# Spreading the weight conversion over the attention pairs of a fused attention, mixer and FFT kernel: fewer steps in pairs 6 to 10, more in the last pair and in the two iterations without scores

## The chip, the cores and the metric

The kernel runs on one core of a Trainium2 chip. The metric is the device time of one execution in microseconds, as the median of several runs. The engines of the core are named as the profile names them: PE is TensorE (matmul, and PEld its weight loads), DVE is VectorE, ACT is ScalarE, POOL is GpSimd, and SP is SyncE, which issues the DMAs.

## The reference

```python
x = attention(q, k, v)      # batch 2, 12 heads, 448 positions, head dim 64, causal, exact softmax
x = moe(x)                  # token mixing 448->256->448 (w_tok1, w_tok2), channel MLP 768->1536->768
x = moe2(x)                 # x + Re(FFT2(x)), layer norm, channel MLP 768->3072->768

def _attn_ref(q, k, v):
    scores = scale * np.matmul(q, k.transpose(0, 1, 3, 2))
    scores = np.where(mask, -1e9, scores)
    attn = softmax(scores)
    return np.matmul(attn, v)

def _moe_ref(x, w_tok1, w_tok2, w_ch1, w_ch2):
    xt = x.transpose(0, 2, 1)
    h = np.maximum(xt @ w_tok1, 0.0) @ w_tok2
    u = x + h.transpose(0, 2, 1)
    h2 = np.maximum(u @ w_ch1, 0.0) @ w_ch2
    return u + h2
```

(Shortened here; the mean and the variance of the layer norm and the two FFTs lie behind the part that the change touches.) The weights reach the kernel as 64-bit floats, and are turned into pairs of 32-bit values (a high part and the rest), with which each product is made in three passes.

## The kernel before

**Attention.** The 12 heads of each of the two batches are taken two at a time: 12 pairs. One loop over n = 0 to 13 is a pipeline of three stages: iteration n makes the scores of pair n (`scores`, PE L261, mask L274, the row maxima on DVE L278, the exps on ACT L287), the transposes of the probabilities of pair n-1 (`transposes`, PE L300, copied out by ACT L305 and DVE L307), and the product with v of pair n-2 (`pv`, PE L315, ACT L320) with its scaling (`finish`, DVE L332, L333, PE L336, DVE L338, L344, POOL L345). `prep` loads and splits q and k of the next pair (ACT L229, L231, POOL L230, DVE L235). In iterations 12 and 13 there are no scores left ("iterations without scores").

**Token mixing inside the same loop.** After every third finished pair, five pieces of token mixing are put on a list, and `next_mix`, called twice an iteration, does the next one: `mix_in` (PE L361, then ACT L367 and DVE L368) with `channels_first` (PE L373, ACT L376), and `mix_out` (PE L395, DVE L397), after which `split` (ACT L401, POOL L402) makes the halves for the channel MLP. The mix_in pieces fall in iterations 5, 8 and 11, and after the loop.

**The channel MLP's beginning.** `early_up(0)` to `early_up(3)` in iterations 12 and 13 are the first four chunks of the MLP's first product (PE L162 to L164, then ACT L165 makes gh, DVE L166 gl), and `early_down(0)` and `early_down(1)` behind the loop the first of its second product (PE L179 to L181 over the four gh and gl, DVE L185). They need weights that have been converted: wa0 to wa3 for early_up, wb0 and wb3 for early_down.

**The conversion.** `convert_steps` turns one tensor of 64-bit words into wh and wl: ACT L83 (m from the words), DVE L85 and L86, DVE L90, DVE L94, ACT L100 (wh), POOL L101 (wl). The generator `converting` does that for eight sources in turn (w1, w2, wa0 to wa3, wb0, wb3), each in three steps, 24 in all: a first with L85 and L86, a second with L90 and with the L83 of the following source, and a third with L94, L100 and L101, after which the source after next is fetched (SP L74) into the buffer of 64-bit words that L94 has just read for the last time. There are two such buffers. wa tensors are 128 x 768, wb tensors 128 x 512.

**What sets the order.** Inside the loop PE runs in the order of the code. The other engines' instructions are put in order by the framework at build time, and each engine then runs its own queue in that order. `weights(after)` does one step of the conversion, to be issued after the instructions given to it. The table `parts` (L461) says how many steps iteration n does; in the pairs' iterations one stands after the first scores, and one more, if there are two, after the third transposes:

```python
parts = [0, 0, 1, 1] + 7 * [2] + [2, 3, 3]
...
if live and parts[n] > 1:
    weights(mark[2:4])
if not live:
    for _ in range(parts[n]):
        weights(mark[:2])
```

Once the loop is over, the rest of the MLP's weights come by the same `convert_steps`, two sources at a time, in the order in which the products need them: wb[0,1] and wb[0,4] are the first two of these.

Of the kernel before, what the change touches and what calls it, by code (L numbers as in the profile page):

```python
# [43 lines left out]
def fused_kernel(ctx: ExitStack, tc: tile.TileContext, qk, v, w1, w2, wa, wb, wc, wd, fa, fa0, fb, out):  # L44
# [27 lines left out]
    def fetch(src):  # L72
        w = stage_pool[0].tile(list(src.shape), I64, tag="w", name="w", bufs=2)
        nc.sync.dma_start(out=w, in_=src)  # L74
        return w
# [111 lines left out]
    with ExitStack() as actx:  # L187
# [24 lines left out]
        mark = [None] * 4  # L212
# [8 lines left out]
        def prep(n):  # L221
            c = Pair()
            pairs[n] = c
            b, hp = n // 6, n % 6
            c.kh, c.kl, c.qh, c.ql = [kq.tile([128, S], F32R, tag=t, name=t) for t in ("kh", "kl", "qh", "ql")]
            k32, q32 = stage(n), stage(n)
            nc.sync.dma_start(out=k32, in_=qk[b, hp, :, 1])
            nc.sync.dma_start(out=q32, in_=qk[b, hp, :, 0])
            act.copy(c.kh, k32)  # L229
            (pool if n else vec).tensor_tensor(out=c.kl, in0=k32, in1=f(c.kh), op=ALU.subtract)  # L230
            act.activation(out=c.qh, in_=q32, func=AF.Copy, scale=0.125)  # L231
            with ExitStack() as order:
                if n == 1:
                    order.enter_context(tc.issue_after(mark[2]))
                vec.scalar_tensor_tensor(  # L235
                    out=c.ql, in0=q32, scalar=0.125, in1=f(c.qh), op0=ALU.mult, op1=ALU.subtract
                )

        def load_v(n):
            pairs[n].v = ap.tile([TS, NI, 2 * D], F32, tag="v", name="v")  # L240
            nc.sync.dma_start(out=pairs[n].v, in_=v[n // 6, n % 6])
# [50 lines left out]
        def transposes(n, u):  # L292
            c = pairs[n]
            if u == 0:
                c.pt = ap.tile([TS, 5, S], F32, tag="pt", name="pt", bufs=1)
            tv = ybank()
            col = 0
            for e, j in (((0, 0),), ((1, 0),), ((0, 1), (0, 3)), ((1, 1), (1, 3)), ((0, 2), (1, 2)))[u]:
                for i in range(j, NI):
                    nc.tensor.transpose(  # L300
                        tv[:TS, col : col + TS], c.p[:, e, OFF[i] + j * TS : OFF[i] + (j + 1) * TS], ident[:TS, :TS]
                    )
                    col += TS
            if u in (1, 3):
                mark[1] = act.copy(c.pt[:, u], tv[:TS, :S]).ins  # L305
            else:
                mark[0] = vec.tensor_copy(c.pt[:, u], tv[:TS, :S]).ins  # L307

        def pv(n):
            c = pairs[n]  # L310
            c.ot = ybank()
            for j in range(NI):
                for e in range(2):
                    u, col = ((e, 0), (2 + e, 0), (4, 224 * e), (2 + e, 336))[j]
                    mm(  # L315
                        c.ot[D * e : D * e + D, j * TS : S], lhsT=c.v[:, j, D * e : D * e + D],
                        rhs=c.pt[:, u, col : col + TS * (NI - j)], start=j == 0, stop=j == NI - 1,
                    )
            c.ots = ap.tile([128, S], F32, tag="ots", name="ots")
            return act.copy(c.ots, c.ot[:, :S]).ins  # L320
# [86 lines left out]
        def next_mix():  # L407
            if mix:
                fn, n, k = mix.pop(0)
                fn(n, k)  # L410
                if fn is mix_out and k == 2:
                    for x in late:
                        split(*x)
                    late.clear()
# [34 lines left out]
        def early_up(fm):  # L449
            up_chunk(None, fm, ahead[fm], (0,), g0, sbank)  # L450

        def early_down(x):
            down_tile([ahead[4 + x]], g0, 0, add_resid, EARLY_DOWN[x], sbank)

        def weights(after):
            with ExitStack() as order:
                for ins in after:
                    order.enter_context(tc.issue_after(ins))
                next(work, None)

        parts = [0, 0, 1, 1] + 7 * [2] + [2, 3, 3]  # L461

        prep(0)
        with tc.manual_schedule(engines={mybir.EngineType.PE}):
            for n in range(np_ + 2):
                live, old = n < np_, 1 <= n <= np_
                if live:
                    scores(n, 0)
                if n + 1 < np_:
                    prep(n + 1)  # L470
                if n in (1, 2):
                    raw.append(fetch(sources[n - 1][0]))
                after = mark[2:4]
                if n >= 2:
                    after.append(pv(n - 2))
                if live and parts[n]:
                    weights(after)
                if live:
                    load_v(n)
                    scores(n, 1)  # L480
                if old:
                    transposes(n - 1, 0)
                    transposes(n - 1, 1)
                next_mix()
                if n == np_:
                    early_up(0)
                if old:
                    transposes(n - 1, 2)
                if live and parts[n] > 1:
                    weights(mark[2:4])  # L490
                if not live:
                    for _ in range(parts[n]):
                        weights(mark[:2])
                if live:
                    scores(n, 2)
                if old:
                    transposes(n - 1, 3)
                    transposes(n - 1, 4)
                if n == np_:
                    early_up(1)  # L500
                next_mix()
                if n == np_ + 1:
                    early_up(2)
                if n >= 2:
                    finish(n - 2)
                if n == np_ + 1:
                    early_up(3)
                if n >= 2 and (n - 2) % 3 == 2:
                    hn = (n - 2) // 3
                    mix += [(mix_first, hn, 0), (mix_second, hn, 1)] + [(mix_out, hn, pr) for pr in range(3)]  # L510
            early_down(0)
            while mix:
                next_mix()
            early_down(1)
# [352 lines left out]
```

## Time and profile before

| | before |
|---|---|
| median of 3 runs | 718.05 us (717.93 to 719.1) |
| the profiled execution's own time | 717.51 us |
| its span | 715.70 us |
| PE busy | 695.1 us (97% of the span) |
| DVE busy | 526.6 us (74%) |
| ACT busy | 282.8 us (40%) |
| POOL busy | 276.7 us (39%) |
| chain that ended last | PE 81%, DVE 10%, ACT 5% |
| fetches of the 64-bit wa and wb tensors, median to landing | 4.3 us and 3.3 us |

The span is what the profiler recorded between the first and the last instruction, and the execution's own time is 1.81 us longer. PE is busy nearly all the time, so the chain of work that ended last runs mostly over PE; a change on another engine counts where PE waits for it. The attention takes about the first 150 us.

### The profile page before, as it was taken

What the parts mean: (1) busy time and instruction counts of PE and PEld (TensorE: products, weight loads), DVE (VectorE), ACT (ScalarE), POOL (GpSimd) and SP (SyncE); (2) the same over time, 40 slices, a digit from 0 to 9 for tenths busy, and PEclk for the clock granted to TensorE, in tenths of its full rate; (3) what the DMA queues carried; (4) which work ended last, traced back from release to release, by engine and by line L of the source; (5) the groups of instructions that cost most, each with busy time, mean ns of one, the idle gap of its engine ahead of it and who ended that gap; (6) DMA issues with size and microseconds to landing.
All of it is one profiled execution on the core that took longest, in us unless ns stands there. A gap on an engine that the chain in (4) does not pass through costs nothing.

```text
span 715.7 us, 10290 instructions
## 1 busy us (share of the span) xinstructions
PE 695.1 (97%) x3940; PEld 629.0 (88%) x3940; DVE 526.6 (74%) x808; ACT 282.8 (40%) x600; POOL 276.7 (39%) x197
## 2 busy tenths in 40 slices
PE   6989899999999999999799999999999999999997
PEld 5677787899999999998699999999999999999996
DVE  6899898554898884779879896767855676944722
ACT  7867777323324333133444452233432323432200
POOL 3235553345332422332195335465313556311210
PEclk9999999999999999999999999999999999999999
DMA  8232412128434342200022442433412343322311
GB/s 265 69 116 96 147 35 82 59 69 224 170 119 147 118 146 90 89 1 0 1 89 88 125 140 90 138 127 118 144 62 81 126 140 126 118 88 95 105 51 52
DMA packets 20608, 74.15 MB, mean 104 GB/s; under 512 B 2364, under 2 KB 6974, under 8 KB 20192
## 3 DMA queue, kind: packets, MB, share of 16 engines
q1 hardware_dynamic: 19952, 69.48, 29.5%
q0 software_dynamic: 608, 4.03, 2.1%
q8 instruction: 31, 0.51, 0.3%
q14 instruction: 17, 0.14, 0.1%
HBM read 70.75 MB, written 2.75 MB: 103 GB/s over the span
## 4 chain that ended last, share of the span: by engine, by line
PE 81%; DVE 10%; ACT 5%; issue 2%; POOL 1%; DMA 0%; ACTq 0%; POOLq 0%; DVEq 0%
PE psum L164 12%; PE psum L163 12%; PE psum L162 12%; PE psum L181 11%; PE psum L180 11%; PE psum L179 11%; PE psum L261 3%; ACT p L287 2%; PE psum L315 2%; PE psum L300 2%; PE psum L395 2%; PE psum L361 1%; DVE nmx L278 1%; DVE resid L655 1%; POOL wl L101 1%
## 5 line engine op out<-in xcount | busy, mean ns | idle before, releaser
L101 POOL TENSOR_TENSOR wl<-m,wh 128x512 fp32r<-128x512 f32 (+1 forms) x90 | 150.1, 1668 | 257.2 <-ACT wh L100 240.6
L180 PE MATMUL psum<-gh,wl 128*128 128x448 f32 x432 | 156.6, 363 | 0.0
L163 PE MATMUL psum<-acth,wl 128*128 128x448 f32 x432 | 156.6, 363 | 0.0
L164 PE MATMUL psum<-actl,wh 128*128 128x448 f32 x432 | 156.4, 362 | 0.0
L181 PE MATMUL psum<-gl,wh 128*128 128x448 f32 x432 | 156.4, 362 | 0.0
L162 PE MATMUL psum<-acth,wh 128*128 128x448 f32 x432 | 156.2, 361 | 0.0
L179 PE MATMUL psum<-gh,wh 128*128 128x448 f32 x432 | 156.2, 361 | 0.0
L83 ACT ACTIVATE m<-w 128x512 f32<-128x512 f32 (+2 forms) x92 | 71.3, 775 | 164.5 <-POOL wl L101 123.1
L85 DVE TENSOR_SCALAR m<-m 128x512 f32<-128x512 f32 (+2 forms) x92 | 48.8, 532 | 77.7 <-ACT m L83 77.6
L90 DVE SCALAR_TENSOR_TENSOR m<-w,m 128x512 uint32<-128x512 uint32 (+2 forms) x92 | 101.6, 1105 | 2.4
L94 DVE SCALAR_TENSOR_TENSOR m<-w,m 128x512 uint32<-128x512 uint32 (+2 forms) x92 | 98.8, 1075 | 1.6
L100 ACT CAST wh<-m 128x512 fp32r<-128x512 f32 (+1 forms) x90 | 63.4, 704 | 90.5 <-DVE m L94 50.2
L162 PEld LDWEIGHTS psum<-acth,wh 128*128 128x128 f32 x432 | 80.9, 187 | 5.8
L163 PEld LDWEIGHTS psum<-acth,wl 128*128 128x128 f32 x432 | 81.1, 188 | 5.6
L180 PEld LDWEIGHTS psum<-gh,wl 128*128 128x128 f32 x432 | 81.1, 188 | 5.6
L179 PEld LDWEIGHTS psum<-gh,wh 128*128 128x128 f32 x432 | 80.9, 187 | 5.8
L164 PEld LDWEIGHTS psum<-actl,wh 128*128 128x128 f32 x432 | 81.0, 188 | 4.8
L181 PEld LDWEIGHTS psum<-gl,wh 128*128 128x128 f32 x432 | 81.0, 187 | 4.8
L166 DVE SCALAR_TENSOR_TENSOR gl<-psum,gh 128x448 fp32r<-128x448 f32 x72 | 43.9, 616 | 25.1 <-ACT gh L165 25.1
L165 ACT ACTIVATE gh<-psum 128x448 fp32r<-128x448 f32 x72 | 37.6, 539 | 61.7 <-PE psum L164 61.7
L86 DVE TENSOR_SCALAR m<-m 128x512 uint32<-128x512 uint32 (+2 forms) x92 | 54.7, 596 | 2.3
L287 ACT ACTIVATE p<-psum,nmx 112x112 f32<-112x112 f32 (+3 forms) x96 | 46.9, 508 | 24.0 <-DVE nmx L278 23.1
(151 smaller groups left out, 855.2 us busy)
## 6 DMA issues: line engine op xcount, KB each, us to landing
w<-in_wc SPq DMA_DIRECT2D x24, 768.0 KB, 4.3
w<-in_wd SPq DMA_DIRECT2D x36, 512.0 KB, 3.4
w<-in_wa SPq DMA_DIRECT2D x12, 768.0 KB, 4.3
w<-in_wb SPq DMA_DIRECT2D x18, 512.0 KB, 3.3
resid<-in_qk SPq DMA_DIRECT2D x24, 224.0 KB, 2.7
v<-in_v SPq DMA_DIRECT2D x12, 224.0 KB, 3.1
out<-t SPq DMA_DIRECT2D x12, 224.0 KB, 1.9
w<-in_w SPq DMA_DIRECT2D x2, 896.0 KB, 9.8
```

The lines of the kernel that those rows point to most:

```text
L83: act.activation(out=m, in_=hi.bitcast(F32), func=AF.Abs)
L90: vec.scalar_tensor_tensor(out=mu, in0=lo, scalar=29, in1=mu, op0=ALU.logical_shift_right, op1=ALU.bitwise_or)
L94: vec.scalar_tensor_tensor(out=mu, in0=hi, scalar=0xC0000000, in1=mu, op0=ALU.bitwise_and, op1=ALU.bitwise_or)
L100: act.copy(wh, m)
L101: pool.tensor_tensor(out=wl, in0=m, in1=f(wh), op=ALU.subtract)
L162: mm(pb[:, :S], lhsT=lh, rhs=act_h[ct][b], start=ct == 0, stop=False)
L163: mm(pb[:, :S], lhsT=ll, rhs=act_h[ct][b], start=False, stop=False)
L164: tail[0] = mm(pb[:, :S], lhsT=lh, rhs=act_l[ct][b], start=False, stop=ct == NCT - 1).ins
L179: mm(pb[:, :S], lhsT=lh, rhs=gh, start=j + k == 0, stop=False)
L180: mm(pb[:, :S], lhsT=ll, rhs=gh, start=False, stop=False)
L181: tail[0] = mm(pb[:, :S], lhsT=lh, rhs=gl, start=False, stop=j == last and k == nk - 1).ins
L287: mark[3] = act.activation(out=c.p[:, e, OFF[i] : OFF[i] + w], in_=se[e][:, c0 : c0 + w], func=AF.Exp, bias=c.nmx[:, i, e], scale=1.0, acc ...
```

## The change

Only the table of the steps and the loop that reads it are changed. The sum stays 24.

| iteration n | 2 | 3 | 4 | 5 | 6 | 7 | 8 | 9 | 10 | 11 | 12 | 13 |
|---|---|---|---|---|---|---|---|---|---|---|---|---|
| steps before | 1 | 1 | 2 | 2 | 2 | 2 | 2 | 2 | 2 | 2 | 3 | 3 |
| steps after | 1 | 1 | 2 | 2 | 1 | 1 | 1 | 1 | 1 | 4 | 6 | 3 |
| done by then, before | 1 | 2 | 4 | 6 | 8 | 10 | 12 | 14 | 16 | 18 | 21 | 24 |
| done by then, after | 1 | 2 | 4 | 6 | 7 | 8 | 9 | 10 | 11 | 15 | 21 | 24 |

```diff
-        parts = [0, 0, 1, 1] + 7 * [2] + [2, 3, 3]
+        parts = [0, 0, 1, 1, 2, 2] + 5 * [1] + [4, 6, 3]
...
-                if live and parts[n] > 1:
-                    weights(mark[2:4])
+                if live:
+                    for _ in range(parts[n] - 1):
+                        weights(mark[2:4])
```

PE's order stays as it was; those of ACT, DVE, POOL and SP change. Three places are shown, with the tiles' numbers.

ACT in iteration 8, up to the L367 of the first half's mix_in there, before; the m and wh tiles are those of the conversion:

```order
L287 ACTIVATE p_1097,ssum_1095<-psum_124,nmx_1096 112x224 x2
L320 COPY ots_1138<-psum_124 128x448
L83 ACTIVATE m_1141<-w_1012 128x768
L305 COPY pt_1158<-psum_124 112x448
L287 ACTIVATE p_1097,ssum_1095<-psum_124,nmx_1096 112x336 x2
L100 CAST wh_1194<-m_921 128x768
L367 ACTIVATE acth4_1_99<-psum_124 128x384
```

After, in the same place:

```order
L287 ACTIVATE p_1088,ssum_1086<-psum_124,nmx_1087 112x224 x2
L320 COPY ots_1129<-psum_124 128x448
L100 CAST wh_1132<-m_719 128x768
L305 COPY pt_1153<-psum_124 112x448
L287 ACTIVATE p_1088,ssum_1086<-psum_124,nmx_1087 112x336 x2
L367 ACTIVATE acth4_1_99<-psum_124 128x384
```

The L83 of a wa tensor is gone from there, and an L100 stands ahead of the exps of 336 columns rather than behind them.

DVE around the boundary of iterations 7 and 8, before (ql and nmx with the higher numbers belong to pairs 9 and 8):

```order
L338 TENSOR_TENSOR x32_823<-psum_124,ssum_673 112x4x128
L235 SCALAR_TENSOR_TENSOR ql_1123<-resid5_1_89,qh_1122 128x448
L344 CAST xh_824<-x32_823 112x4x128
L347 COPY x32_823<-x32_823 112x4
L278 TENSOR_REDUCE nmx_1096<-psum_124 112x2
```

After:

```order
L397 TENSOR_TENSOR resid2_0_82<-psum_124,resid2_0_82 128x448
L307 COPY pt_1022<-psum_124 112x448
L235 SCALAR_TENSOR_TENSOR ql_1114<-resid5_1_89,qh_1113 128x448
L278 TENSOR_REDUCE nmx_960<-psum_124 112x2
L307 COPY pt_1022<-psum_124 112x448
L338 TENSOR_TENSOR x32_823<-psum_124,ssum_673 112x4x128
L344 CAST xh_824<-x32_823 112x4x128
L347 COPY x32_823<-x32_823 112x4
L278 TENSOR_REDUCE nmx_1087<-psum_124 112x2
```

The L235 has moved ahead of a row maximum, a copy and the L338 of the iteration before.

DVE in iteration 11, up to the L368 of the second half's mix_in, before (m_1345 is a wa tensor's):

```order
L278 TENSOR_REDUCE nmx_1517<-psum_124 112x2 x2
L90 SCALAR_TENSOR_TENSOR m_1345<-w_1198,m_1345 128x768
L278 TENSOR_REDUCE nmx_1517<-psum_124 112x2
L307 COPY pt_1569<-psum_124 112x448
L94 SCALAR_TENSOR_TENSOR m_1345<-w_1198,m_1345 128x768
L368 SCALAR_TENSOR_TENSOR actl4_1_111<-psum_124,acth4_1_99 128x384
```

After (m_1005 belongs to wa1, m_1417 to wa2):

```order
L278 TENSOR_REDUCE nmx_1496<-psum_124 112x2 x2
L94 SCALAR_TENSOR_TENSOR m_1005<-w_774,m_1005 128x768
L278 TENSOR_REDUCE nmx_1496<-psum_124 112x2
L307 COPY pt_1552<-psum_124 112x448
L85 TENSOR_SCALAR m_1417<-m_1417 128x768
L86 TENSOR_SCALAR m_1417<-m_1417 128x768
L90 SCALAR_TENSOR_TENSOR m_1417<-w_1136,m_1417 128x768
L94 SCALAR_TENSOR_TENSOR m_1417<-w_1136,m_1417 128x768
L368 SCALAR_TENSOR_TENSOR actl4_1_111<-psum_124,acth4_1_99 128x384
```

Between the L307 and the L368 stand four conversion operations instead of one. On ACT, the order after has L83 of wa3 directly ahead of the L367 that belongs to this L368:

```order
L320 COPY ots_1528<-psum_124 128x448
L100 CAST wh_1531<-m_1005 128x768
L305 COPY pt_1552<-psum_124 112x448
L287 ACTIVATE p_1497,ssum_1495<-psum_124,nmx_1496 112x336 x2
L83 ACTIVATE m_1590<-w_1535 128x768
L367 ACTIVATE acth4_1_99<-psum_124 128x384
```

Before, an L100 stood there, and the L83 stood further up.

ACT in iteration 13, before (w_2082 is wb[0,1], w_2146 is wb[0,4]; gh_1814 and gh_1848 are those of early_up(2) and early_up(3)):

```order
L83 ACTIVATE m_2084<-w_2082 128x512
L320 COPY ots_1791<-psum_124 128x448
L83 ACTIVATE m_2148<-w_2146 128x512
L401 CAST acth2_1_95<-resid2_1_83 128x448
L165 ACTIVATE gh_1814<-psum_124 128x448
L165 ACTIVATE gh_1848<-psum_124 128x448
```

After (m_1728 is that of wb3):

```order
L320 COPY ots_1791<-psum_124 128x448
L83 ACTIVATE m_1728<-w_1723 128x512
L83 ACTIVATE m_2084<-w_2082 128x512
L401 CAST acth2_1_95<-resid2_1_83 128x448
L100 CAST wh_1810<-m_1728 128x512
L165 ACTIVATE gh_1814<-psum_124 128x448
L83 ACTIVATE m_2148<-w_2146 128x512
L165 ACTIVATE gh_1848<-psum_124 128x448
```

wb3's L83 and L100 have come into this stretch, and the L83 of wb[0,4] stands between the two gh.

DVE in iteration 13 and behind it, after:

```order
L85 TENSOR_SCALAR m_1728<-m_1728 128x512
L397 TENSOR_TENSOR resid2_1_83<-psum_124,resid2_1_83 128x448
L86 TENSOR_SCALAR m_1728<-m_1728 128x512
L90 SCALAR_TENSOR_TENSOR m_1728<-w_1723,m_1728 128x512
L94 SCALAR_TENSOR_TENSOR m_1728<-w_1723,m_1728 128x512
L338 TENSOR_TENSOR x32_1646<-psum_124,ssum_1495 112x4x128
L166 SCALAR_TENSOR_TENSOR gl_1815<-psum_124,gh_1814 128x448
...
L85 TENSOR_SCALAR m_2148<-m_2148 128x512
L90 SCALAR_TENSOR_TENSOR m_2084<-w_2082,m_2084 128x512
L86 TENSOR_SCALAR m_2148<-m_2148 128x512
L94 SCALAR_TENSOR_TENSOR m_2084<-w_2082,m_2084 128x512
L166 SCALAR_TENSOR_TENSOR gl_1849<-psum_124,gh_1848 128x448
```

Before, wb3's four operations stood ahead of the L166 of early_up(1), an iteration half earlier.

## Rows read from the trace of the kernel before

**Rows 1.** Busy by stretch: us, PE, PEld, DVE, ACT, POOL, PEclk, DMA, GB/s.

```profile
122.00:156.00 34.00, 34.00 (x207) 30.07 (x205) 20.85 (x41) 12.32 (x25) 13.63 (x10) 1.00 0.15 47
156.00:289.00 133.00, 133.00 (x671) 124.72 (x671) 99.94 (x139) 45.08 (x72) 44.08 (x31) 1.00 0.44 141
```

**Rows 2.** PE's waits, 56 to 165 us: total us, times, longest.

```profile
PE psum L300 <- DVE actl L368: 2.0, 2, 1.6
PE psum L336 <- DVE resid L397: 0.6, 2, 0.3
```

**Rows 3.** Timeline in iteration 7: start, us, engine, line, [idle before <-releaser].

```profile
73.71 0.55 DVE L85 TENSOR_SCALAR m<-m 128x768 f32<-128x768 f32 x1
74.15 1.83 POOL L101 TENSOR_TENSOR wl<-m,wh 128x768 fp32r<-128x768 f32 x1 [1.21 <-ACT wh L100]
74.29 2.10 DVE L86 TENSOR_SCALAR m<-m 128x768 uint32<-128x768 uint32 x1
...
76.98 0.65 PE L336 MATMUL psum<-ident,ots 128*112 128x128 f32 x4 [0.29 <-DVE resid L397]
```

**Rows 4.** Timeline in iteration 8, with its mix_in.

```profile
79.51 0.82 DVE L235 SCALAR_TENSOR_TENSOR ql<-resid,qh 128x448 fp32r<-128x448 f32 x1
...
82.70 0.35 ACT L287 ACTIVATE p<-psum,nmx 112x112 f32<-112x112 f32 x1 [2.57 <-DVE nmx L278]
...
84.63 0.97 ACT L83 ACTIVATE m<-w 128x768 f32<-128x768 f32 x1
...
86.92 0.88 ACT L100 CAST wh<-m 128x768 fp32r<-128x768 f32 x1
87.64 0.55 ACT L367 ACTIVATE acth<-psum 128x384 fp32r<-128x384 f32 x1
...
88.84 0.59 PE L300 MATMUL psum<-ident,p 112*112 112x112 f32 x4 [1.60 <-DVE actl L368]
```

**Rows 5.** Timeline in iteration 11, with its mix_in.

```profile
115.20 1.16 DVE L90 SCALAR_TENSOR_TENSOR m<-w,m 128x768 uint32<-128x768 uint32 x1
...
117.58 0.94 DVE L94 SCALAR_TENSOR_TENSOR m<-w,m 128x768 uint32<-128x768 uint32 x1
...
120.10 0.53 ACT L367 ACTIVATE acth<-psum 128x384 fp32r<-128x384 f32 x1
...
121.27 0.60 PE L300 MATMUL psum<-ident,p 112*112 112x112 f32 x4 [0.40 <-DVE actl L368]
```

**Rows 6.** DMA issues of the fetches: count, KB each, median us to landing.

```profile
w<-in_wa SPq DMA_DIRECT2D x12, 768.0 KB, 4.3
w<-in_wb SPq DMA_DIRECT2D x18, 512.0 KB, 3.3
```

**Rows 7.** Timeline in iterations 12 and 13 and behind the loop.

```profile
134.58 0.42 DVE L85 TENSOR_SCALAR m<-m 128x512 f32<-128x512 f32 x1
...
138.37 0.69 DVE L94 SCALAR_TENSOR_TENSOR m<-w,m 128x512 uint32<-128x512 uint32 x1
...
141.40 1.33 POOL L402 TENSOR_TENSOR actl<-resid,acth 128x448 fp32r<-128x448 f32 x1
...
151.19 0.62 DVE L166 SCALAR_TENSOR_TENSOR gl<-psum,gh 128x448 fp32r<-128x448 f32 x1
...
152.58 0.36 PE L181 MATMUL psum<-gl,wh 128*128 128x448 f32 x1
```

**Rows 8.** Timeline in iteration 6: DVE's conversion beside POOL.

```profile
60.80 1.29 POOL L345 TENSOR_TENSOR xl<-x,xh 112x512 fp32r<-112x512 f32 x1 [3.56 <-DVE xh L344]
61.38 1.12 DVE L85 TENSOR_SCALAR m<-m 128x768 f32<-128x768 f32 x1
```

**Rows 9.** Timeline of PE: its wait ahead of L315 near 46 us.

```profile
46.01 0.79 PE L315 MATMUL psum<-pt,v 112*64 112x224 f32 x8 [1.70 <-DVE pt L307]
```

**Rows 10.** Busy by stretch (as Rows 1) behind the waits of Rows 9 and 4.

```profile
47.40:50.90 3.50, 3.50 (x21) 3.40 (x17) 3.47 (x8) 2.53 (x10) 1.28 (x1) 0.51 0.41 131
88.00:91.40 3.40, 2.56 (x16) 2.54 (x17) 3.17 (x5) 2.17 (x6) 3.20 (x2) 1.00 0.39 154
```

## The prediction

> **What bounds the kernel now.** I read the busy time by stretch first. From 122 to 289 us TensorE (PE) is busy in every microsecond, at full clock [rows 1], so whatever moves its start at 156 us moves the end of that stretch by as much, and the stages behind it start from there. The change touches only the conversion of weights ahead of about 150 us, so its effect is the sum of what it does to PE's waits up to there. The second view is PE's waits in that part: two waits at L300 for L368, 2.0 us together with 1.6 the longest, and two at L336 for L397, 0.6 together [rows 2]. Each has conversion work in front of the operation that PE waits for. The stretch from 122 to 156 us has no wait to remove, and a new one can only cost.
>
> **Gain 1, pairs 7 and 10.** PE's L336 waits for DVE's L397, and ahead of L397 on DVE stands an L86 that took 2.10 us while POOL's L101 ran beside it [rows 3]. With one part in a pair only one step of a converted tensor is left in it; by the new order L85 and L86 fall elsewhere and L397 is met without them. I count both waits as gone: 2 x 0.3 = 0.6 us by the grouped row [rows 2], 0.56 by the single ones (0.29 and 0.27).
>
> **Gain 2, pair 8, the first mix_in.** The chain behind PE's 1.60 us is L287 (exps) on ACT, L100, L367, then L368 on DVE [rows 4]. Before, ACT has an L83 (0.97) and an L100 (0.88) between the first exps and L367; after, one L100, moved ahead of two exps, and no L83. One conversion operation less is 0.72 us by the starts of L100 and L367 (86.92 to 87.64). The first exps had waited 2.57 us for L278, and an L235 of 0.82 us stands on DVE ahead of that L278 [rows 4]; in the new order it is one position group earlier, in pair 7. Together 0.72 + 0.82 = 1.54 of the 1.60. Floor: 0.72, if L278 is not reached sooner. Ceiling: 1.60, all of the wait. I take 1.55. The gains are 0.56 + 1.55 = 2.11 us, between 1.3 and 2.2.
>
> **Loss 1, pair 11, the second mix_in.** Before, DVE has one L94 (0.94, starting at 117.58) between an L307 and L368, and PE waits 0.40 us at L300 for L368 [rows 5]. The parts spared up to pair 10 are made up here: by the new order L85, L86, L90 and L94 of wa2 stand between that L307 and L368. That is 0.55 + 0.55 + 0.94 + 0.94 = 3.0 us (0.55 is an undisturbed L85 of this size [rows 3], and I take the same for L86; 0.94 is the L94's row, taken for L90 too), so L368 can't start before about 117.58 + 3.0 = 120.6, or 122.1 if this L86 too meets an L101 and takes 2.10 [rows 3]; the L94 of 0.94 that stood there before belongs to these four now. On ACT, L83 of wa3 now stands directly ahead of L367. It waits for wa3's fetch, issued only when wa1's L94 has freed the buffer, and by the new order that L94 has the place where an L90 ran from 115.20 to 116.36 [rows 5]; with 4.3 us to land [rows 6] if the L94 ends between 115.4 and 116.4 (it is the shorter operation, and may start late), the L83 starts at 119.7 to 120.7, and L367, 0.7 us behind it as L367 was behind L100 [rows 4], at 120.4 to 121.4 against 120.10 before [rows 5]. So L368 runs 0.3 to 1.4 us later than before (by ACT 0.3 to 1.3, by DVE from nothing to 122.1 less 120.7, 0.56 behind L367's old start), and PE, which already waits there, waits as much longer. I take 0.7, the middle of the fetch's case, with an undisturbed L86.
>
> **Loss 2, the iterations without scores.** The parts still add up to 24, but the tail's share comes later by one source. Before, wb0 and wb3 are converted together there (DVE from 134.58 to 139.06 [rows 7]), both buffers come free, and the two fetches that follow are issued about 138 and 139. After, that place holds wa3 and wb0: two operations more of the wider form, about 5.2 us instead of 4.5, still before anything that PE needs. But wb3 is left. Its fetch is issued at about 138.7, when wa3's L94 ends; 3.3 us later [rows 6] it has landed, at about 142.0; its L83 ends about 142.8. Its L85 and L86 (0.42 each [rows 7]), L90 and L94 (0.69 each [rows 7]) and one L397 (0.6, for which I take L166's row of the same tile) between them end at 142.8 + 2.8 = 145.6 if nothing disturbs DVE. In that stretch POOL now runs wa3's L101 (1.83 [rows 3]), wb0's (two thirds of that, about 1.2, for two thirds of the columns), L402 (1.33 [rows 7]) and L345 (1.29 [rows 8]), nearly back to back from 139.6 to 146 by their order. A DVE operation beside POOL work takes longer in this trace: an L85 of 128x768 took 1.12 us when it started 0.6 us into an L345 of 1.29 [rows 8], twice the 0.55 of an undisturbed one, and the L86 of [rows 3] 2.10 beside a POOL operation of 1.83. If the four wait behind the POOL work, the last ends at about 148.9 at the latest. I take 148.2, near the late end, since both rows show a DVE operation ending only after the POOL operation has.
>
> [...]
>
> The next fetch, wb[0,4], needs that buffer: issued at 148.2, landed at 151.5, its L83 (0.67) ends at 152.2. By the new order this L83 stands on ACT ahead of L165 (gh) of early_up(3), and L85, L86, L90 and L94 of the neighbouring tensors, about 2.0 us with 0.62 for L166 itself behind them, stand ahead of that chunk's gl on DVE. So gl ends about 152.2 + 0.2 + 2.0 + 0.6 = 155.0. PE's L181 that reads it started at 152.58 before, with L166 started at 151.19 [rows 7]. PE then waits 155.0 - 152.6 = 2.4; I take 2.3, some 0.8 of it at L179 for gh and the rest at L181. With wb3 done at 148.9 it is 3.1 (up to 3.2 with rounding), with wb3 done at 145.6 the chain ends at 152.4, and the wait is nothing. L338 and L344 of the same iterations move behind wb3's operations too; PE reads their tiles only after that L181. The moved fetches on SP stand ahead of nothing else than each other there, since no q, k or v is left to load.
>
> **Sum.** -2.11 + 0.7 + 2.3 = +0.9 us. PE has no gap from 156 to 289 us, so all of it arrives at the end: profiled 717.51 (span 715.70 and 1.81 around it) to 718.4. That execution lies 0.54 below the median of 718.05, so the forecast for the median is 718.9. Bounds: with gains of 1.3 and losses of 1.4 + 3.2 it is +3.3; with 2.2 and 0.3 + 0 it is -1.9.
>
> **Rivals.**
> [...]
> *POOL out of the way (faster).* If wb3's four DVE operations pass before or between the POOL operations, wb[0,4] is fetched by about 146 and its chain ends ahead of PE: loss 2 is gone, and 718.05 - 2.11 + 0.7 = 716.6. For it: POOL is not full in that stretch (13.63 us busy of 34 [rows 1]), and the four operations need only 2.2 us. Against: they come just when two L101 have been released.
> *The pair-11 wait is the larger one, or pair 8 keeps its own (slower).* If wa3's fetch is issued as late as the present L94's end, 118.52 [rows 5], its L83 starts at 122.8 and L367 a microsecond later: 3.7 us lost instead of 0.7, 721.9. If L235's move brings nothing and pair 8 keeps 0.9 of its wait, 719.7.
>
> **How the numbers follow.** About 0.2% (1.44 us) is what a measurement of this kernel tells from no change: under 716.6 is faster, over 719.5 slower. The forecast case has 0.40, with a range of its own of 717.4 to 720.2; about a quarter of it lies over 719.5. The clock rival has 0.25, all slower. POOL out of the way has 0.28, half of it under 716.6. The third has 0.07, all slower. Slower: 0.10 + 0.25 + 0.07 = 0.42, faster 0.14, the same 0.44. The range runs from 716.2, the bound of -1.9 on the median, to 720.9, which takes in the clock rival and leaves out the third and the worst bounds.
>
> **What would show it.** Right, step by step: no wait at L336 for L397 in pairs 7 and 10; at L300 in pair 8 under 0.3 us; in pair 11 about 1.1 us at L300, with an L83 directly ahead of L367; a new PE wait at L179 or L181 between 150 and 155 us that L165 or L166 releases, with the L83 of wb[0,4] around 152. If PE shows no wait between 122 and 156 us, loss 2 was wrong, and the time is at most 717.3; if the granted clock falls after 152 us, the clock rival has come. A wait that comes up in pairs 5 to 7, where I see none, would make the whole sum wrong.

## The result, and the profile after

| | before | after |
|---|---|---|
| median | 718.49 us (4 runs, 717.93 to 719.1) | 722.44 us (4 runs, 721.32 to 723.81) |
| ratio to before | | 1.0056, 95% interval 1.0035 to 1.0077 |
| profiled execution | 717.51 us, span 715.70 | 722.9 us, span 720.8 |

The change made the kernel slower by 0.56%, some 4 us. The forecast was 718.9 with a range up to 720.9: the sign of the sum was right, the size was not, and the time lies outside the range. The median of before is of four runs here; the forecast started from the 718.05 of the first three. Line numbers of the kernel after are those of before up to L491 and one higher behind it, which touches none of the lines below.

PE's waits between 56 and 165 us, after, as [rows 2] shows them for before:

```profile
PE psum L300 <- DVE actl L368: 2.1, 2, 1.3
PE psum L181 <- DVE gl L166: 1.5, 1, 1.5
PE psum L179 <- ACT gh L165: 0.4, 1, 0.4
PE psum L373 <- ACT ots L320: 0.3, 1, 0.3
```

The two waits at L336 for L397 are gone. L300's two waits for L368 are still there, in other sizes (in iteration 8 0.78 for 1.60, in iteration 11 1.34 for 0.40), and two waits are new, at the first L179 that reads early_up(3)'s gh and at the L181 that reads its gl.

The busy time of the stretches of [rows 1], after (us, PE, PEld, DVE, ACT, POOL, PEclk, DMA, GB/s):

```profile
122.00:156.00 34.00, 32.17 (x189) 27.56 (x188) 26.34 (x44) 12.83 (x26) 14.46 (x11) 0.99 0.20 65
156.00:289.00 133.00, 133.00 (x669) 124.92 (x668) 96.27 (x135) 45.17 (x72) 44.70 (x31) 0.99 0.45 144
```

PE lost 1.83 us in the first of them, where it had waited for nothing before, and its clock is no longer 1.00 in either. The next view places both. Three milestones of PE: the first L179 (early_down(0)), the first L361 behind it (mix_first) and the first L162 of the MLP proper. Before:

```profile
150.38 0.36 PE L179 MATMUL psum<-gh,wh 128*128 128x448 f32 x1
...
152.79 0.86 PE L361 MATMUL psum<-xh,w1h 112*128 112x384 f32 x4
...
164.25 0.36 PE L162 MATMUL psum<-acth,wh 128*128 128x448 f32 x1
```

After:

```profile
150.21 0.36 PE L179 MATMUL psum<-gh,wh 128*128 128x448 f32 x1
...
155.00 1.40 PE L361 MATMUL psum<-xh,w1h 112*128 112x384 f32 x4
...
168.00 0.36 PE L162 MATMUL psum<-acth,wh 128*128 128x448 f32 x1
```

PE reaches the first L179 0.17 us earlier than before: that is all that is left of the gains once iteration 11 is paid. From L179 to L361 it takes 4.79 us instead of 2.41, so loss 2 cost 2.38: 1.83 of waits that the view counts, and 0.55 around them. The first matmul behind each wait takes 0.47 us instead of 0.36, its weight load starting only with it (both at 152.56 and both at 154.69; 0.20 us ahead of the matmul at the first L179), and matmuls without a wait between them start every 0.20 us although each is recorded with 0.36. From L361 to L162 it takes 13.00 instead of 11.46: the same matmuls, 1.54 us longer, at a lower clock (PEclk 0.50 from 156 to 158 us, where it was 1.00 before). Together the kernel after is 3.75 us late there. The last matmul ends 4.91 us late (715.88 for 710.97): the remaining 1.16 came in the FFT stage, behind a wait of 4.04 us that both kernels have (it ends at 353.6 us before and at 357.3 after), where the clock stayed low longer after. The 10 us behind that wait, before:

```profile
353.50:358.50 5.00, 4.92 (x18) 4.33 (x19) 3.07 (x10) 3.04 (x7) 2.22 (x2) 0.66 0.00 0
358.50:363.50 5.00, 5.00 (x26) 4.64 (x25) 2.93 (x6) 2.68 (x6) 4.98 (x6) 1.00 0.08 10
```

After, from where the wait ends there:

```profile
357.30:362.30 5.00, 4.97 (x14) 4.33 (x15) 2.86 (x9) 2.30 (x6) 1.41 (x2) 0.50 0.00 0
362.30:367.30 5.00, 5.00 (x24) 4.56 (x24) 2.52 (x6) 2.39 (x5) 4.69 (x5) 0.90 0.00 0
```

The chain of loss 2 ran as the prediction had it, after:

```profile
142.66 0.41 DVE L85 TENSOR_SCALAR m<-m 128x512 f32<-128x512 f32 x1
...
144.06 1.49 POOL L345 TENSOR_TENSOR xl<-x,xh 112x512 fp32r<-112x512 f32 x1
...
144.42 2.79 DVE L90 SCALAR_TENSOR_TENSOR m<-w,m 128x512 uint32<-128x512 uint32 x1
...
145.51 1.15 POOL L402 TENSOR_TENSOR actl<-resid,acth 128x448 fp32r<-128x448 f32 x1
...
147.24 0.69 DVE L94 SCALAR_TENSOR_TENSOR m<-w,m 128x512 uint32<-128x512 uint32 x1
...
151.40 0.67 ACT L83 ACTIVATE m<-w 128x512 f32<-128x512 f32 x1 [2.38 <-DMA w<-in_wb]
151.98 0.53 ACT L165 ACTIVATE gh<-psum 128x448 fp32r<-128x448 f32 x1
...
154.03 0.61 DVE L166 SCALAR_TENSOR_TENSOR gl<-psum,gh 128x448 fp32r<-128x448 f32 x1
```

wb3's L90 took 2.79 us beside two POOL operations that follow each other (its L94, of the same size, 0.69), wb3 was done at 147.9, wb[0,4] landed at about 151.3, its L83 kept L165 waiting on ACT, and gl was there at 154.6.

One sign by which the prediction called its whole sum wrong did come up, just ahead of the view that begins at 56 us: a wait in iteration 5, whose steps are the same in both kernels. After (the first row in the columns of [rows 1], PEclk third from the right):

```profile
47.40:50.90 3.50, 3.50 (x31) 3.31 (x26) 3.46 (x8) 2.54 (x10) 1.29 (x1) 1.00 0.41 131
```

```profile
54.59 0.60 PE L300 MATMUL psum<-ident,p 112*112 112x112 f32 x4 [1.21 <-DVE actl L368]
54.95 0.95 PE L361 MATMUL psum<-xh,w1h 112*128 112x384 f32 x4
```

Before, in the same place:

```profile
54.94 0.96 PE L361 MATMUL psum<-xh,w1h 112*128 112x384 f32 x4
```

After the wait of 1.70 us near 46 us PE ran at half clock in the execution of before (0.51, [rows 10]) and at full clock here (1.00). At full clock it came early to L300 and waited there for L368 (0.28 us for L307 as well, at 51.37), and it was at the next L361 at the same time as before. DVE's L368 starts at 53.96 us before and at 53.97 after. So this wait adds nothing to the change's cost, and the half clock of before had cost nothing there: it was not PE that set the pace.

### The profile page after: what moved, and what is told of

It reads as the page before. It is cut to its first block, busy times and chain, and to the rows that moved or that the text cites. A ratio compares the mean times of both kernels' runs of the same rounds, so it can differ in the third digit from the quotient of the medians.

```text
span 720.8 us, 10287 instructions
## 1 busy us (share of the span) xinstructions
PE 696.8 (97%) x3940; PEld 629.4 (87%) x3940; DVE 529.2 (73%) x808; ACT 283.0 (39%) x600; POOL 273.5 (38%) x197
## 4 chain that ended last, share of the span: by engine, by line
PE 80%; DVE 12%; ACT 3%; issue 2%; POOL 1%; DMA 0%; ACTq 0%; DVEq 0%; POOLq 0%
PE psum L163 12%; PE psum L164 12%; PE psum L162 11%; PE psum L181 11%; PE psum L180 11%; PE psum L179 10%; PE psum L261 3%; PE psum L300 2%; PE psum L315 2%; PE psum L395 2%; PE psum L361 2%; DVE m L90 2%; ACT p L287 2%; DVE nmx L278 1%; DVE m L94 1%
## 5 line engine op out<-in xcount | busy, mean ns | idle before, releaser
L101 POOL TENSOR_TENSOR wl<-m,wh 128x512 fp32r<-128x512 f32 (+1 forms) x90 | 150.3, 1671 | 256.9 <-ACT wh L100 243.4
L181 PE MATMUL psum<-gl,wh 128*128 128x448 f32 x432 | 156.5, 362 | 1.5 <-DVE gl L166 1.5
L180 PE MATMUL psum<-gh,wl 128*128 128x448 f32 x432 | 156.6, 363 | 0.0
L179 PE MATMUL psum<-gh,wh 128*128 128x448 f32 x432 | 156.3, 362 | 0.4 <-ACT gh L165 0.4
L162 PE MATMUL psum<-acth,wh 128*128 128x448 f32 x432 | 156.2, 361 | 0.0
L83 ACT ACTIVATE m<-w 128x512 f32<-128x512 f32 (+2 forms) x92 | 71.2, 774 | 167.0 <-POOL wl L101 128.8
L90 DVE SCALAR_TENSOR_TENSOR m<-w,m 128x512 uint32<-128x512 uint32 (+2 forms) x92 | 102.5, 1115 | 2.5
L94 DVE SCALAR_TENSOR_TENSOR m<-w,m 128x512 uint32<-128x512 uint32 (+2 forms) x92 | 98.3, 1069 | 1.6
L100 ACT CAST wh<-m 128x512 fp32r<-128x512 f32 (+1 forms) x90 | 63.2, 704 | 90.2 <-DVE m L94 50.8
L181 PEld LDWEIGHTS psum<-gl,wh 128*128 128x128 f32 x432 | 81.0, 187 | 6.6 <-DVE gl L166 1.8
L179 PEld LDWEIGHTS psum<-gh,wh 128*128 128x128 f32 x432 | 80.9, 187 | 6.6 <-ACT gh L165 0.8
L180 PEld LDWEIGHTS psum<-gh,wl 128*128 128x128 f32 x432 | 81.1, 188 | 5.6
L162 PEld LDWEIGHTS psum<-acth,wh 128*128 128x128 f32 x432 | 80.9, 187 | 5.7
L166 DVE SCALAR_TENSOR_TENSOR gl<-psum,gh 128x448 fp32r<-128x448 f32 x72 | 43.8, 616 | 25.4 <-ACT gh L165 25.4
L165 ACT ACTIVATE gh<-psum 128x448 fp32r<-128x448 f32 x72 | 37.6, 539 | 60.8 <-PE psum L164 60.8
L86 DVE TENSOR_SCALAR m<-m 128x512 uint32<-128x512 uint32 (+2 forms) x92 | 53.6, 584 | 2.3
```

What stands on the lines that cost most here:

```text
L83: act.activation(out=m, in_=hi.bitcast(F32), func=AF.Abs)
L90: vec.scalar_tensor_tensor(out=mu, in0=lo, scalar=29, in1=mu, op0=ALU.logical_shift_right, op1=ALU.bitwise_or)
L94: vec.scalar_tensor_tensor(out=mu, in0=hi, scalar=0xC0000000, in1=mu, op0=ALU.bitwise_and, op1=ALU.bitwise_or)
L100: act.copy(wh, m)
L101: pool.tensor_tensor(out=wl, in0=m, in1=f(wh), op=ALU.subtract)
L162: mm(pb[:, :S], lhsT=lh, rhs=act_h[ct][b], start=ct == 0, stop=False)
```

## The experiments

Four questions: does the loss sit in the tail or in the pairs; what does the wait cost by itself and what the clock behind it; does the clock's fall belong to the program; and can the gains be had without the losses. Each kernel was timed in turn with the kernel before on the same chip; kernels that were timed on different chips are compared by their ratios.

**The tail alone.** The pairs keep two steps, and iterations 12 and 13 get the late tail:

```diff
-        parts = [0, 0, 1, 1, 2, 2] + 5 * [1] + [4, 6, 3]
+        parts = [0, 0, 1, 1, 2, 2, 2, 2, 2, 2, 1, 0, 6, 3]
```

> The tail of the change alone: the steps of iterations 6 to 9 are as before, iteration 10 has one and 11 none, and iterations 12 and 13 have six and three, so that the queues of DVE and ACT from iteration 12 on read as in the changed kernel. Theory (the loss sits in the tail: a wait of 1.8 us at L179 and L181 for gh and gl of early_up(3), then about 2 us of PE work at half clock, as in the trace after): about 0.7 us gained in iterations 10 and 11, then 3.9 lost: 721 to 722, with the same two PE waits and a granted clock near 0.5 right behind them. Rival (the loss sits in the pairs, and the clock's fall is chance): 717.5 to 719.

Measured: 721.64 us, ratio 1.0040 (1.0024 to 1.0056). Most of the loss is the tail's, as the theory had it, and the same two waits are there (0.27 and 1.42 us). One part of the expectation failed: in this trace the clock did not fall behind them (the stretch from 154 to 160 us, PEclk in the third column from the right; the kernel after ahead of it for comparison).

```profile
154.00:160.00 6.00, 5.31 (x23) 5.26 (x24) 3.02 (x6) 0.92 (x2) 0.00 (x0) 0.72 0.57 175
```

```profile
154.00:160.00 6.00, 4.31 (x25) 3.65 (x24) 4.58 (x9) 1.23 (x4) 0.04 (x1) 1.00 0.40 112
```

This execution had its falls elsewhere: behind the wait of 1.61 us in iteration 8, which it shares with the kernel before, PEclk was 0.63:

```profile
92.00:95.60 3.60, 3.60 (x20) 3.41 (x18) 2.09 (x5) 2.46 (x7) 0.63 (x1) 0.63 0.22 64
```

**The wait taken away.** The changed kernel, where the conversions of wb[0,1] and wb[0,4] are issued after gh and gl of early_up(3):

```diff
-            act.activation(out=gh, in_=pb[:, :S], func=AF.Relu)
-            vec.scalar_tensor_tensor(
+            last_g[0] = act.activation(out=gh, in_=pb[:, :S], func=AF.Relu).ins
+            last_g[1] = vec.scalar_tensor_tensor(
...
                 if n == np_ + 1:
                     early_up(3)
+                    hold.extend(last_g)
```

> The changed kernel, with the conversions of wb[0,1] and wb[0,4] put behind gh and gl of early_up(3) on ACT and DVE, by two more instructions that they are issued after; nothing else is moved. Theory: the wait at L179 and L181 is gone and the clock stays at 1.00 from 150 to 170 us: 718.5 - 1.1 + 0.9 = 718.3, 717.8 to 719. Rival 1 (gh and gl come late of themselves, since wb3's four DVE operations are late): a wait of over 0.8 us stays, 719.5 to 722. Rival 2 (the two conversions come too late for the products behind the loop): a new PE wait at an L179 behind 160 us, over 720.

Measured: 719.63 us, ratio 1.0008 (0.9994 to 1.0023). No wait of PE from 122 us to the FFT stage, and no fall of the clock from 122 to 340 us (PEclk 1.00). So what the tail cost, wait and clock together, is the step from 1.0056 to 1.0008, some 3.4 us, and it hung on where these conversions stood in the queues: an L83 that waits for its DMA, ahead of an L165 on ACT, with DVE operations of the conversions ahead of L166. The time lies over the expected 717.8 to 719, but the kernel before took 719.09 beside it and not the 718.5 of that sum; the interval takes in the -0.2 us (0.9998) that PE's lead at the first L179 in the changed kernel promises.

**The wait filled with work.** The changed kernel with matmuls that nothing reads in the place of the wait:

```diff
+            spare = psum[:, 4 + 2 * (turn["s"] % 2) + 1]
+            for _ in range(9):
+                mm(spare[:, :S], lhsT=ahead[0][0][:, :128], rhs=act_h[0][0], start=True, stop=True)
             early_down(0)
```

> The changed kernel, with nine matmuls of 448 columns that nothing reads put ahead of early_down(0) on PE, about 1.8 us of work in the place of the wait. It separates the wait from what the clock does behind it. Theory (the clock's fall behind the wait costs 2 us): the waits at L179 and L181 shrink to under 0.3 us, the clock stays at 1.00, and the time is 2 us under that of the changed kernel: 720 to 721. Rival (the clock's fall has another cause, or costs nothing in the end): the time is that of the changed kernel, 722 to 723.

Measured: 721.69 us, ratio 1.0042 (1.0028 to 1.0055). The wait at L181 fell to 0.41 us and the clock stayed at 1.00 from 122 to 340 us. By the ratios the time is about 1.0 us under the changed kernel's, not 2, and the intervals overlap: right in direction, too small to be called shown. The two traces alone show what the clock cost: from L361 to L162 11.47 us here against 13.00.

**The kernel before, a second trace; the kernel after, a second trace.** No edit.

> The kernel before, once more, for a second trace of it. Theory (whether the clock falls behind a wait of 1.6 to 1.7 us changes from one execution of the same program to the next, each fall being worth about 1.5 us in the end): this trace shows its halves of the clock at another set of the waits than the first one (behind the waits near 4, 46, 89 and 353 us), and its time differs from 717.5 by about 1.5 us for each more, with the same waits of PE up to 122 us. Rival (the falls belong to the program): half clock at 47 to 51 and 354 to 358 us again, nowhere else, and 717.5.

> The changed kernel, once more, for a second trace and a ratio on the same chip as the others. Theory: the ratio again near 1.005; the waits at L179 and L181 again 0.4 and 1.5 us; the clock's fall behind them comes in most executions and not in all. Rival: the fall behind 155 us is there in each execution, which would make it a fixed part of the change's cost.

Measured: before 717.52 us, with the same waits and a lower clock at the same two places as in the first trace (PEclk 0.88 from 46 to 60 us and 0.72 from 352 to 358 us in both). By itself that is the rival, and the theory's own sign did not come. But the 25 executions of it beside the first four experiments lie between 717.49 and 720.62, and its two traces are of the lowest ones. The mean granted clock of each of the 25 was recorded: the six at 0.995 took 717.49 to 719.09 us, the eight at 0.989 to 0.992 720.01 to 720.62. So the executions at the lower mean clock were the slower ones; where in them it fell, no trace shows. After: 723.43 us, ratio 1.0058 (1.0037 to 1.0078), with waits of 0.74 and 1.44 us in the tail and again half clock behind them (0.50 from 156 to 159 us); its first waits are those of the first trace, yet here the clock also fell at the start of the attention (0.89 from 4 to 20 us, 1.00 in the first trace). So in both traces of the kernel after the fall came behind the tail's wait, and in the kernel with the tail alone (and one more below) much the same wait did not.

**Three steps in iterations 6 and 9**, to spare 7 and 10 with the old tail:

```diff
+        parts = [0, 0, 1, 1, 2, 2, 3, 1, 2, 3, 1, 2, 3, 3]
```

> Three steps in iterations 6 and 9, one in 7 and 10, two in 8 and 11, and the tail as before (three and three): the two pairs with the L336 wait are spared without any work left for the tail. Theory (the gains of the change sit in pairs 7 and 10, 0.3 to 0.5 us each, and the tail as before costs nothing): 717.4 to 718.2, no PE wait at L336 for L397, L300's waits for L368 as before (1.6 and 0.4). Rival (the third step of iterations 6 and 9 stands ahead of their L397 or L307 on DVE and makes PE wait): 718.6 to 720.

Measured: 723.03 us, ratio 1.0058 (1.0037 to 1.0079): the rival, and beyond its 718.6 to 720. L397 keeps PE waiting no longer, but PE waits twice at L300 for ACT's L320:

```profile
PE psum L300 <- ACT ots L320: 4.5, 2, 2.3
PE psum L300 <- DVE actl L368: 0.8, 1, 0.8
```

The third step puts its L94 in front of the row maxima on DVE, and its L101 on POOL beside the L344 and L332 that stand ahead of the next pair's first row maxima:

```profile
69.34 2.80 POOL L101 TENSOR_TENSOR wl<-m,wh 128x768 fp32r<-128x768 f32 x1
...
70.38 2.05 DVE L344 CAST xh<-x 112x512 fp32r<-112x512 f32 x1
```

L344 took 2.05 us here and 0.43 before, L332 1.10 and 0.16. So the exps of the next pair began at 74.59 instead of 71.27, and L320 stands behind them on ACT.

**The tail alone, held.** The kernel with the tail alone and the hold:

> The kernel with the tail alone (one step in iteration 10, none in 11, six and three), and the conversions of wb[0,1] and wb[0,4] held behind gh and gl of early_up(3). Theory (that kernel lost its 2.9 us by the wait at L179 and L181 and what the clock did behind it): the wait is gone and 0.7 us is left of gain, 717.8 to 718.8, ratio 0.998 to 1.0. Rival (its loss was chance in the clock at the start and behind the wait of iteration 8): no more than 1 us better than the kernel with the tail alone, over 720.

Measured: 718.01 us, ratio 0.9988 (0.9976 to 1.0000), as the theory had it, some 3.7 us better by the ratios than without the hold (1.0040). With iterations 10 and 11 emptied the waits at 111 and 121 us are gone in its trace; the two of iterations 7 and 8 (0.29 and 1.62) stay.

**One step in 7, 8 and 10, the rest spread, and the hold:**

```diff
+        parts = [0, 0, 1, 1, 2, 2, 2, 1, 1, 2, 1, 2, 6, 3]
```

> One step in iterations 7, 8 and 10, two in 6, 9 and 11, six and three in 12 and 13, and the conversions of wb[0,1] and wb[0,4] held behind gh and gl of early_up(3). Theory: the gains of the change stay (0.5 in iteration 7, some 0.2 in 8, 0.45 in 10), iteration 11 is as before with 0.4 at L300, no wait in the tail: 1.1 us under the kernel before, and a shorter wait in iteration 8, behind which the clock falls less often: 717 to 718. Rival (what iteration 9 and 11 take up gives new waits at L300 or L315): 718.5 to 720.

Measured: 716.33 us, ratio 0.9956 (0.9942 to 0.9970). PE's only wait between 56 and 165 us is

```profile
PE psum L374 <- ACT ots L321: 0.3, 1, 0.3
```

and its gain is larger than expected, since the wait in iteration 8 is gone altogether: PE is at the first L179 (L180 here) at 147.53 us instead of 150.38, and at its last matmul's end at 708.12 instead of 710.97, 2.85 earlier both times. Iteration 8 also settles gain 2. ACT's way from the first exps of iteration 8 to L367 (here L368, the lines being one higher), after:

```profile
82.88 0.35 ACT L287 ACTIVATE p<-psum,nmx 112x112 f32<-112x112 f32 x1 [2.26 <-DVE nmx L278]
...
84.81 0.86 ACT L100 CAST wh<-m 128x768 fp32r<-128x768 f32 x1
...
87.01 0.53 ACT L367 ACTIVATE acth<-psum 128x384 fp32r<-128x384 f32 x1
...
88.19 0.60 PE L300 MATMUL psum<-ident,p 112*112 112x112 f32 x4 [0.78 <-DVE actl L368]
```

and in this kernel, where no conversion operation stands between the two:

```profile
82.32 0.35 ACT L288 ACTIVATE p<-psum,nmx 112x112 f32<-112x112 f32 x1 [2.25 <-DVE nmx L279]
...
85.71 0.53 ACT L368 ACTIVATE acth<-psum 128x384 fp32r<-128x384 f32 x1
```

Before it took 4.94 us (82.70 to 87.64, [rows 4]) with two conversion operations, after 4.13 with one, here 3.39 with none: 0.74 to 0.81 each. PE's wait was 1.60, 0.78 and 0.

**The same without the hold.**

> The steps of the kernel that was 0.9956 of the time before (one in iterations 7, 8 and 10, two in 6, 9 and 11, six and three in 12 and 13), without the hold on wb[0,1] and wb[0,4]. Theory (the late tail costs a wait of 1.7 to 1.9 us at L179 and L181, and in most executions half clock behind it): 716.3 + 1.8 + 1 to 2 = 719 to 720.2, with that wait in the trace and none from 60 to 150 us over 0.4. Rival (the gain of that kernel came from its pairs alone, and the hold is worth nothing here): 716 to 717.

Measured: 718.64 us, ratio 0.9993 (0.9983 to 1.0003), 2.7 us (0.37%) more than with the hold, a little under the theory's 719 to 720.2. Its waits are 0.48 and 1.42 us, and the clock stayed at 1.00:

```profile
147.59 0.36 PE L179 MATMUL psum<-gh,wh 128*128 128x448 f32 x1
...
152.45 0.87 PE L361 MATMUL psum<-xh,w1h 112*128 112x384 f32 x4
...
163.92 0.36 PE L162 MATMUL psum<-acth,wh 128*128 128x448 f32 x1
```

From L179 to L361 4.86 us as in the kernel after, and from L361 to L162 11.47 as before. The wait is the fixed part of the tail's price, about 2.4 us; the clock's part of up to 1.5 us came on top in both traces of the kernel after and in neither of this one and the tail alone.

**One step more moved forward, from iteration 4 to 3**, on the best kernel so far:

```diff
-        parts = [0, 0, 1, 1, 2, 2, 2, 1, 1, 2, 1, 2, 6, 3]
+        parts = [0, 0, 1, 2, 1, 2, 2, 1, 1, 2, 1, 2, 6, 3]
```

> The kernel that was 0.9956 of the time before, with one step moved from iteration 4 to iteration 3: L94 of w1 an iteration earlier, and L85 and L86 of w2 ahead of the last row maxima of iteration 4. It asks whether the wait of 1.70 us at L315 near 46 us, which all kernels so far share, is that same L86 (3.79 us beside POOL's L101 of w1) ahead of L307. Theory: yes; the L86 takes under 1.5 us, the wait at L315 falls under 0.5, and the time goes down by 0.5 to 1.7 us: 714.6 to 716. Rival (DVE, busy 19 of 20 us there, has no room: the wait moves to an L261 or L300 nearby): 716 to 718.

Measured: 713.99 us, ratio 0.9926 (0.9913 to 0.9938), better than expected, and better than both kernels. L86 of w2 took 0.63 us:

```profile
35.19 3.23 POOL L101 TENSOR_TENSOR w1l<-m,w1h 112x1024 fp32r<-112x1024 f32 x1 [0.26 <-ACT w1h L100]
...
40.57 0.63 DVE L86 TENSOR_SCALAR m<-m 128x896 uint32<-128x896 uint32 x1
```

and POOL's L101 was over by then, at 38.42 us. Before, where it met L101 and the POOL operation behind that (L230, up to 43.95), it took six times as long:

```profile
40.23 2.62 POOL L101 TENSOR_TENSOR w1l<-m,w1h 112x1024 fp32r<-112x1024 f32 x1 [4.05 <-ACT w1h L100]
...
40.62 3.81 DVE L86 TENSOR_SCALAR m<-m 128x896 uint32<-128x896 uint32 x1
```

The wait of 1.70 us ahead of L315 [rows 9] is gone, and the half clock behind it too (PEclk from 46 to 60 us 1.00, without this step 0.88). Waits of 0.35 (at an earlier L316), 0.69 (at an L262) and 0.63 us (at an L301) are in the trace instead; PE is 1.1 us earlier at the first L179 than in the kernel without this step (146.39 for 147.53), although in this execution the clock was low at the start of the attention (0.89 from 4 to 20 us, without this step 1.00). The medians are 2.3 us apart. The rest goes with the mean granted clock: of the six executions without this step the two at 0.995 took 714.76 and 714.83 us and the four at 0.991 to 0.993 716.33 to 716.76, while all five with it had 0.994 or 0.995 and took 713.51 to 714.31. Why the clock fell less with it isn't shown.

## Why the prediction was wrong, point by point

**Gain 1** was right: both L336 waits went. PE started iteration 8 0.50 us earlier (77.06 for 77.56), and iteration 10 gave 0.45, against 0.56 for both, since a wait costs PE more than the idle time that the view counts.

**Gain 2 was mis-sized, and it is the step of the sum that failed most**: 1.55 forecast; PE gained 0.15 over the whole of iteration 8. The term had two parts. One conversion operation less on ACT was worth 0.81 (0.72 forecast). The other, 0.82 for the moved L235, was nothing. The move brought L235 forward, but not earlier work to do: it stood waiting for its qh, and held up what had come behind it (after):

```profile
77.04 1.20 DVE L235 SCALAR_TENSOR_TENSOR ql<-resid,qh 128x448 fp32r<-128x448 f32 x1 [1.35 <-ACT qh L231]
...
78.16 1.08 DVE L278 TENSOR_REDUCE nmx<-psum 112x2 f32<-112x896 f32 x1
79.16 0.61 DVE L307 COPY pt<-psum 112x448 f32<-112x448 f32 x1
...
82.15 0.61 DVE L278 TENSOR_REDUCE nmx<-psum 112x2 f32<-112x448 f32 x1
```

That L307 ends so late that the L315 behind it took 2.46 us instead of 2.11; at the first L361 of iteration 8 nothing is left of the 0.50 won in iteration 7 (82.29 for 82.17), and the exps began 0.18 us later than before, not 0.8 earlier. An operation that is moved forward frees time only if its own input is there. The prediction's floor, 0.72, was the value to take, and its last rival named this very case ("L235's move brings nothing and pair 8 keeps 0.9 of its wait", 719.7), inside a chance of 0.07.

**Loss 1** was right within its bounds: the wait in iteration 11 grew by 0.94 (0.7 forecast, 0.3 to 1.4). The fetch landed in time; what the prediction kept for its upper case, an L86 that meets an L101, came true:

```profile
116.11 2.00 POOL L101 TENSOR_TENSOR wl<-m,wh 128x768 fp32r<-128x768 f32 x1 [2.74 <-ACT wh L100]
...
116.45 2.08 DVE L86 TENSOR_SCALAR m<-m 128x768 uint32<-128x768 uint32 x1
...
119.15 0.92 ACT L83 ACTIVATE m<-w 128x768 f32<-128x768 f32 x1 [1.63 <-DMA w<-in_wa]
119.55 0.96 DVE L94 SCALAR_TENSOR_TENSOR m<-w,m 128x768 uint32<-128x768 uint32 x1
119.96 0.49 ACT L367 ACTIVATE acth<-psum 128x384 fp32r<-128x384 f32 x1
120.48 0.56 DVE L368 SCALAR_TENSOR_TENSOR actl<-psum,acth 128x384 fp32r<-128x384 f32 x1
```

L368 starts when DVE's L94 (120.51) and ACT's L367 (120.45) have both ended, so neither way alone sets it. It is not later than before, as the prediction's words have it, but 0.18 us earlier (120.48 for 120.66); PE comes there 1.12 us earlier (its L300 ahead of the wait starts at 119.16 for 120.28) and waits the 0.94 longer. Most of what the pairs had gained by then is spent there.

**Loss 2** was right in its steps and its size: 2.38 us at L361 against 2.3, by way of the very steps of the text, each within some 0.4 us. A DVE operation beside POOL's took longer here too: the L90 2.79 us beside POOL's L345 and L402, an L90 of the same size 0.68 at 152.49 with no POOL operation beside it, and the L86 of w2 above once 3.81 and once 0.63 us. The long L90 started 0.36 us into L345 and ended at 147.21, 0.55 us behind L402's end. What makes it longer, no run here shows.

**The clock** was named as a rival, at 0.25, and the range takes it in; it came, for 1.54 us. No run shows a price that such a fall always has, or a length of wait that brings it; in their place the runs showed this. A wait of 1.45 us behind one of 0.38 and one of 1.44 behind one of 0.74 were followed by half clock in the two traces of the kernel after (0.50 in both), and waits of 1.42 us behind 0.27 in the kernel with the tail alone and behind 0.48 in the spread one were followed by 1.00; and the wait of 1.70 at L315, followed by half clock in the kernel before (0.51, [rows 9, 10]), was followed by 1.00 in the kernel after. So the length of a wait does not decide it here. Nor was the price one value: rows 10 show work at half clock, and there, as iteration 5 above shows, PE would have waited anyway. In the tail PE had nothing to wait for behind it, and the 1.54 reached the end; the second trace has 1.27.

**The range** added each rival to the forecast by itself. Here two came at once, pair 8 and the clock: 719.7 and the measured 1.54 are 721.2, already over its upper end of 720.9. By the measured terms the sum is -0.95 - 0.15 + 0.94 + 2.38 = +2.2 us instead of +0.9, of which 1.4 is the error in iteration 8: 720.3 for the median, inside the range. The clock's 1.54 in the tail and the 1.16 in the FFT stage make up most of what is left: 717.51 + 2.2 + 1.54 + 1.16 = 722.4 of the profiled 722.9 (of the other 0.5 some 0.2 lie between PE's last matmul and the end of the span, and 0.3 outside the span). That adds up for one execution of each. In the medians the clock's part is less sure: 717.51 is near the lowest of the kernel before, whose 25 executions above have a median of 719.09.

## What to carry to other kernels

An instruction that waits for a late DMA must not stand in a queue ahead of work that the busiest engine reads (here an L83 after 2.38 us of waiting, with the L165 behind it at 151.98 and PE waiting 0.38 us for that at L179); look at the first conversions behind a stage as well as at the stage itself. Holding two such conversions back was worth 2.7 to 3.7 us in three pairs of kernels here. When an operation is moved forward in a queue, look for its own inputs first: if they aren't there, everything behind it pays. And a DVE operation that takes long beside POOL's is the one to move, by an iteration if need be: L86 took 3.81 us beside L101 and L230 and 0.63 without them, and PE was 1.1 us earlier for it. Half clock is worth removing where PE sets the pace, as in the tail, where it cost 1.54 and 1.27 us; where another engine does, as in iteration 5 here, it cost nothing.

## What the runs showed of the hardware that was not expected

Half clock behind a PE wait was no fixed property of the wait here. With much the same waits the stretch of it came in one execution and not in another: behind the 1.70 us near 46 us, in iterations whose steps are the same, in both traces of the kernel before (PEclk 0.88 from 46 to 60 us) and in neither of the kernel after (1.00). In the tail it cost 1.54 and 1.27 us where it came (L361 to L162 13.00 and 12.73 us in the two traces of the kernel after, instead of 11.46) and nothing where it didn't (11.47); near 46 us it cost nothing. Behind the FFT stage's wait of 4.0 us the clock fell in every trace (the lower of PEclk from 352 to 358 and from 358 to 362 us is 0.50 to 0.84 in the twelve), but not for the same time: the part from the last stretch of L179 to L181 in the first MLP (289.05 us before) to the last matmul, which none of the kernels changes, took 421.9 us in both traces of the kernel before and in the two fastest kernels, and 422.6 to 423.4 us in the others, both traces of the kernel after among them. What decides that, no run here shows. The executions of one kernel spread over 3 us, as wide as most changes to it, so that a single trace of before and one of after differ by several such stretches on top of what the change did.
